# First FFN2 of a fused attention and SwiGLU kernel: one plain output tile instead of three, with the weight sums between the products of the first group

## The chip, the cores and the metric

The kernel runs on one core of one Trainium2 chip. The metric is the device time of one execution in microseconds; lower is better. Seven runs of the kernel before are given by their median, and one further execution was recorded by the hardware profiler.

## The reference, cut to what matters

```python
# q, k, v: (8 batches, 12 heads, 448 tokens, 64) in float32
scores = q @ k.T / sqrt(64) - log(448)
attn   = sigmoid(scores) @ v                      # per batch and head
x      = attn.transpose(0, 2, 1, 3).reshape(3584, 768)
g      = x @ w_gate                               # 768 x 1536
val    = x @ w_val
out    = (g * sigmoid(g) * val) @ w_out           # 1536 x 768, out is (3584, 768) float32
```

The last product, with `w_out`, is called FFN2 here. The two products before it, with the gate, are FFN1.

## The kernel before, in words

**Stages.** The eight batches are taken in four pairs `pb` = 0 to 3, each of 896 tokens. For each of the first three pairs TensorE runs 24 FFN1 units (`ffn1`, 12 blocks of 128 columns of d_ff for each of the two batches), and then FFN2 for the pair. The last pair has a different FFN1 (`ffn1_pair`), and then its FFN2. The attention of later batches is cut into steps (`attn_step`: three or four score chunks of one quad of heads, with `pv`, the product with v, of the quad before) and put between these units.

**FFN2.** A pair has 7 output tiles of 128 tokens by 768 columns. There are two ways to make them. `ffn2` makes one tile plainly: 12 blocks of d_ff by two halves of 384 columns, 24 matmuls. `ffn2_group` makes two tiles, g and g + 3, by a Strassen-like scheme with 7 products of 6 matmuls each, 42 matmuls for what would plainly be 48. The products are made in the order 1, 2, 6, 5, 7, 3, 4, in turn into the two banks of one PSUM tile, and after each VectorE moves the bank to an output buffer (`snap`, line 567) or adds it to what is there (`put`, line 573). The scheme needs sums of blocks of the hidden activations (`hS`, made on VectorE by `make_sums`, line 515) and sums of blocks of `w_out` (`wT`, made on VectorE by `w_sum(s, kind)`, line 484, s for one half of d_ff). Product 6 needs `wT` of kind 2, product 5 of kind 1, product 7 of kind 3 and product 4 of kind 4, each for s = 0 and, three matmuls later, for s = 1. Kind 2 is computed from kind 3, and kind 4 from kind 2. The weight sums are made once, in the FFN2 of pair 0, and used by all groups.

**The FFN2 of pair 0 before.** Its units are: `make_sums(99)` (all hidden sums still queued), `ffn2` of tile 6, four weight sums (s = 0), `ffn2` of tile 0, four weight sums (s = 1), `ffn2` of tile 3, and the groups g = 1 and g = 2. Pairs 1 to 3 have `ffn2` of tile 6 and three groups.

**Order of the work.** The whole order of instructions is fixed by the program: nothing is rescheduled. A list `units` holds the units with a planned duration each (`FU1`, `FU2`, `FU3`), and a running planned time `tcur` decides where each attention step is put: it goes ahead of the next unit once its due time `vtime` is reached. The due times are spread over the planned time up to `LAST`, the planned end of FFN1 of batch 5. Each `ffn1` of an odd batch makes some of the queued hidden sums on VectorE; how many (`budget`) depends on how soon an attention step follows.

**PSUM and buffers.** Eight banks form a ring of four tiles of two banks (`ring`). Each score chunk, each `pv`, each `ffn1`, each `ffn2` and each group takes the next tile of the ring (`Banked`). A matmul that starts a bank waits until the readers of that bank by its last user are done; the other bank does not matter. Output buffers `osb` come from a pool of four, and are stored by DMAs on SyncE's queue; the casts of q and k are on GpSimd.

## Time and profile before

| what | value |
| --- | --- |
| median of 7 runs | 410.87 us (409.89 to 413.54) |
| profiled execution, its own time | 409.85 us |
| its span from the first to the last instruction | 408.0 us |
| TensorE busy (share of the span) | 396.7 us (97%) |
| VectorE busy | 258.7 us (63%) |
| ScalarE busy | 231.7 us (57%) |
| GpSimd busy | 169.8 us (42%) |
| matmuls of plain FFN2 tiles, line 614 | 144 of 326 ns |
| matmuls of groups, line 556 | 462 of 326 ns |
| weight sums, line 484 | 8, seven of about 750 ns, one of 1485 ns |

The table counts 144 plain matmuls (six tiles of 24) and 462 in groups (eleven groups of 42). Matmuls overlap in TensorE's pipeline, so the mean of one is longer than the distance between two. The granted TensorE clock is 1.000 for the whole span.

### The profile page before, as it was taken

The page shows a single profiled execution, that of the slowest core. Times are in us where ns is not written, and L with a number is a line of the kernel's source. Part 1 is how long each engine was busy: PE and PEld are TensorE (multiplying, and loading weights), DVE is VectorE, ACT ScalarE, POOL GpSimd, SP SyncE. Part 2 cuts the span into 40 slices and gives each one's busy share as a digit, 9 for nine tenths or more (in the row PEclk, how much of TensorE's full clock was granted, in tenths as well). Part 3 has the DMA queues.
Part 4 walks back from the last instruction along what each step waited for, and adds up shares of the span by engine and source line. Part 5 has one row for each costly group of instructions (what it writes and reads, how often), then busy time and mean ns, then how long its engine had stood idle before and what let it go on. Part 6 is the DMA issues. An engine that isn't in the chain of part 4 may idle for free.

```text
span 408.0 us, 8021 instructions
## 1 busy us (share of the span) xinstructions
PE 396.7 (97%) x3158; PEld 206.2 (51%) x3158; DVE 258.7 (63%) x463; ACT 231.7 (57%) x333; POOL 169.8 (42%) x209
## 2 busy tenths in 40 slices
PE   7799999999999999999999999999999999999995
PEld 3444544545555444444555544445455555555563
DVE  2637647688955554767755555558786557777753
ACT  5966885744355667575444476685565435666000
POOL 3628042353433333331203043400039999999000
PEclk9999999999999999999999999999999999999999
DMA  8999956959899968872437897810002520000135
GB/s 260 251 249 251 236 95 119 199 119 211 213 207 269 218 158 154 170 141 100 112 80 169 232 174 164 181 34 15 1 2 53 141 80 0 2 1 0 40 83 148
DMA packets 59844, 54.38 MB, mean 133 GB/s; under 512 B 35744, under 2 KB 53280, under 8 KB 59808
## 3 DMA queue, kind: packets, MB, share of 16 engines
q0 software_dynamic: 18880, 30.94, 34.1%
q1 hardware_dynamic: 40496, 22.62, 24.8%
q8 instruction: 24, 0.39, 0.4%
q10 hardware_dynamic: 432, 0.33, 0.3%
q14 instruction: 12, 0.10, 0.1%
HBM read 47.19 MB, written 11.01 MB: 143 GB/s over the span
## 4 chain that ended last, share of the span: by engine, by line
PE 87%; DVE 5%; ACT 3%; DMA 3%; issue 1%; SPq 0%; POOL 0%; DVEq 0%; ACTq 0%
PE ps_D L296 39%; PE ps_D L556 19%; PE ps_D L403 11%; PE ps_D L230 8%; PE ps_D L262 6%; PE ps_D L614 4%; DMA v<-in_v_dram 2%; ACT pt L248 2%; DVE S L515 2%; DMA st<-in_q_dram 1%; PE ps_D L200 1%; DVE t L316 1%; DVE hT L320 1%; ACT pt L245 1%; DVE hT L428 0%
## 5 line engine op out<-in xcount | busy, mean ns | idle before, releaser
L248 ACT ACTIVATE pt<-ps_D,sb_t 128x896 f16<-128x896 f32 x148 | 140.1, 1017 | 74.6 <-PE ps_D L230 69.9
L296 PE MATMUL ps_D<-xT,wg 128*128 128x448 f16 x432 | 95.3, 353 | 0.1
L296 PE MATMUL ps_D<-xT,wv 128*128 128x448 f16 x432 | 94.8, 352 | 0.0
L181 POOL CAST c<-st 128x896 bf16<-128x896 f32 x41 | 38.3, 937 | 134.6 <-DMA st<-in_q_dram 84.7
L316 DVE TENSOR_TENSOR t<-ps_D,s 128x448 f16<-128x448 f32 x72 | 44.7, 622 | 58.6 <-ACT s L314 58.6
L296 PEld LDWEIGHTS <-wg 128*128 128x128 f16 x432 | 39.5, 98 | 44.9 <-issue 12.1
L296 PEld LDWEIGHTS <-wv 128*128 128x128 f16 x432 | 42.2, 98 | 39.5 <-issue 0.4
L314 ACT ACTIVATE s<-ps_D 128x448 f16<-128x448 f32 x72 | 39.5, 549 | 38.9 <-PE ps_D L296 28.3
L320 DVE SCALAR_TENSOR_TENSOR hT<-ps_D,t 128x448 f16<-128x448 f32 x72 | 45.0, 625 | 7.5
L230 PE MATMUL ps_D<-T,T 64*64 64x448 bf16 x644 | 44.4, 357 | 2.4 <-DVE T L206 1.2
L567 DVE TENSOR_SCALAR osb<-ps_D 128x384 f32<-128x384 f32 x43 | 24.0, 558 | 20.2 <-PE ps_D L556 19.0
L262 PE MATMUL ps_D<-pt,v 64*64 64x448 f16 x672 | 36.0, 350 | 0.4 <-DMA v<-in_v_dram 0.4
L556 PEld LDWEIGHTS <-S 128*128 128x128 f16 x264 | 25.8, 98 | 17.1
L556 PE MATMUL ps_D<-wT,S 128*128 128x384 f16 x198 | 34.0, 326 | 0.0
L230 PEld LDWEIGHTS <-T 64*64 64x64 bf16 x644 | 15.0, 105 | 25.1 <-issue 18.2
L271 DVE CAST xT<-ps_D 128x448 f16<-128x448 f32 x24 | 15.0, 625 | 19.8 <-PE ps_D L262 15.6
L573 DVE SCALAR_TENSOR_TENSOR osb<-ps_D,osb 128x384 f32<-128x384 f32 x33 | 18.4, 558 | 13.5 <-PE ps_D L556 13.5
L262 PEld LDWEIGHTS <-v 64*64 64x64 f16 x672 | 19.5, 107 | 13.2 <-issue 0.9
L556 PEld LDWEIGHTS <-hT 128*128 128x128 f16 x198 | 18.7, 98 | 14.6 <-issue 2.9
L276 DVE CAST xT<-ps_D 64x448 f16<-64x448 f32 x41 | 25.5, 621 | 0.7
L614 PE MATMUL ps_D<-wo,hT 128*128 128x384 f16 x144 | 24.4, 326 | 0.5 <-DVE hT L428 0.3
L556 PE MATMUL ps_D<-wo,hT 128*128 128x384 f16 x132 | 23.3, 326 | 0.0
(80 smaller groups left out, 427.5 us busy)
## 6 DMA issues: line engine op xcount, KB each, us to landing
out_dram<-osb SPq DMA_DIRECT2D x52, 192.0 KB, 2.9
st<-in_q_dram POOLq DMA_DIRECT2D x20, 448.0 KB, 6.0
st<-in_k_dram POOLq DMA_DIRECT2D x20, 448.0 KB, 7.3
v<-in_v_dram POOLq DMA_DIRECT2D x24, 224.0 KB, 5.2
wg<-in_moe_w_gate_dram POOLq DMA_DIRECT2D x4, 576.0 KB, 12.3
wv<-in_moe_w_val_dram POOLq DMA_DIRECT2D x4, 576.0 KB, 12.8
wo<-in_moe_w_out_dram POOLq DMA_DIRECT2D x4, 576.0 KB, 6.7
st<-in_q_dram SPq DMA_DIRECT2D x3, 448.0 KB, 7.6
```

The source lines that it names most:

```text
L181: eng.tensor_copy(out=t.rearrange("p c h d -> p h c d"), in_=st.rearrange("p h (c d) -> p h c d", c=C))
L230: nc.tensor.matmul(out=sc[w * 64:(w + 1) * 64, h2, :S], lhsT=kt[r, w * 64:(w + 1) * 64], rhs=qt[r, :, w * 64:(w + 1) * 64], start=True, st ...
L248: nc.scalar.activation(out=pt, in_=sc[:, :, :S], func=SIGM, bias=sb_t, scale=qkscale)
L262: nc.tensor.matmul(out=P[g:g + 64, h2, :S], lhsT=vt[r, h2, c * D:(c + 1) * D], rhs=pt[r, h2, :], start=(c == 0), stop=(c == C - 1),)
L276: done = [nc.vector.tensor_copy(out=o, in_=i) for o, i in halves[how:]]
L296: nc.tensor.matmul(out=D.t[:, i, :S], lhsT=(wg16, wv16)[i][f // FW][:, pr, cs], rhs=xT[(b, pr)], start=(pr == 0), stop=(pr == NP - 1),),
L314: D.read(nc.scalar.activation(out=s16, in_=D.t[:, 0, :S], func=SIGM), 0)
L316: D.read(nc.vector.tensor_tensor(out=t1, in0=D.t[:, 0, :S], in1=s16, op=MULT), 0)
L320: nc.vector.scalar_tensor_tensor(out=hT[(b // 2, f)][:, b % 2, :], in0=D.t[:, 1, :S], scalar=HSC, in1=t1, op0=MULT, op1=MULT),
L403: nc.tensor.matmul(out=D[kind].t[:, bank, :S], lhsT=l, rhs=r, start=(first and i == 0), stop=(i == NP // 2 - 1), skip_group_check=True,),
L556: nc.tensor.matmul(out=D.t[:, bank, :hw], lhsT=l, rhs=B_(i), start=(first and i == 0), stop=(i == HF - 1), skip_group_check=True,),
L614: nc.tensor.matmul(out=D.t[:, half, :hw], lhsT=h[:, m * 128:(m + 1) * 128], rhs=wo16[f // FW][:, f % FW, half * hw:(half + 1) * hw], start ...
```

## The change

In the FFN2 of pair 0, tiles 0 and 3 are no longer made plainly but by a group g = 0, as in the other pairs. The eight weight sums are spread differently: kinds 3 and 2 for both s go ahead of `ffn2` of tile 6, kind 1 for s = 0 goes behind it (and behind the attention step that follows it), and the other three go into the group g = 0, behind its products 2, 5 and 7. `ffn2_group` gets an argument for them. As the planned duration of the stage is different, the due times of the later attention steps are computed anew.

```diff
-    def ffn2_group(pb, g):
+    def ffn2_group(pb, g, between):
...
+        def extra(k):
+            if k in between:
+                w_sum(*between[k])
+
...
         mm(2, 1, True, True)
         put(1, o1, 0)
+        extra(2)
...
         mm(5, 1, True, False)
         o2 = osp.tile([128, DM], FP32, tag="osb", name="osb")
         snap(1, o2, 1)
+        extra(5)
         mm(7, 0, False, False)
         put(0, o2, 1)
+        extra(7)
...
         o_units = [(0.0, make_sums, (99,)), (FU2, ffn2, (pb, C - 1))]
+        between = {}
         if pb == 0:
 
-            ts = [(0.0, w_sum, (s, kind)) for s in range(2) for kind in (3, 2, 1, 4)]
-            o_units += ts[:4] + [(FU2, ffn2, (pb, 0))] + ts[4:] + [(FU2, ffn2, (pb, 3))]
-        for g in range(1 if pb == 0 else 0, 3):
-            o_units.append((FU3, ffn2_group, (pb, g)))
+            ts = [(0.0, w_sum, (s, kind)) for s in range(2) for kind in (3, 2)]
+            o_units = o_units[:1] + ts + o_units[1:] + [(0.0, w_sum, (0, 1))]
+            between = {2: (1, 1), 5: (0, 4), 7: (1, 4)}
+        for g in range(3):
+            o_units.append((FU3, ffn2_group, (pb, g, between if g == 0 else {})))
```

## The prediction

> **What bounds the kernel now.** I read the page first: TensorE (PE) is busy for 97% of the span, and the chain that ended last is PE for 87% of it. So PE time is end time, unless PE waits.

> ```profile
> span 408.0 us, 8021 instructions
> PE 396.7 (97%) x3158; PEld 206.2 (51%) x3158; DVE 258.7 (63%) x463; ACT 231.7 (57%) x333; POOL 169.8 (42%) x209
> PE 87%; DVE 5%; ACT 3%; DMA 3%; issue 1%; SPq 0%; POOL 0%; DVEq 0%; ACTq 0%
> ```

> An average hides stages, so next I read the chain of waits over the stage that is edited, FFN2 of pair 0, from 98 us (columns: start, length, what).

> ```profile
> 98.99 0.62 DVE hT L320
> 99.61 0.97 DVE S L515
> ...
> 102.05 0.08 DVE S L515
> 102.13 0.19 issue
> 102.33 0.56 DVE osb L627
> 102.89 0.04 issue
> 102.93 7.96 PE ps_D L614 x48
> 110.89 0.50 PE ps_D L230 x8
> ...
> 113.09 6.93 PE ps_D L556 x42
> ```

> At the entry of this stage the chain is on VectorE (DVE), not on PE. The last gate (L320) is followed by six hidden sums (L515), and only then by the move of tile 6 out of PSUM (L627); when that ends at 102.89, PE starts tile 0 at 102.93. From there to 298 us the chain is PE without a gap worth naming: what is lost here isn't made up later. The timeline of the same stage gives durations and what else DVE does:

> ```profile
> 102.33 1.01 DVE L627 TENSOR_SCALAR osb<-ps_D 128x384 f32<-128x384 f32 x2
> 102.93 7.96 PE L614 MATMUL ps_D<-wo,hT 128*128 128x384 f16 x48 [0.18 <-DVE osb L627]
> 103.26 0.75 DVE L484 TENSOR_TENSOR wT<-wo,wo 128x1152 f16<-128x1152 f16 x1
> 104.04 0.76 DVE L484 TENSOR_TENSOR wT<-wT,wo 128x1152 f16<-128x1152 f16 x1
> 104.72 0.75 DVE L484 TENSOR_TENSOR wT<-wo 128x1152 f16<-128x1152 f16 x1
> 109.02 1.12 POOL L181 CAST c<-st 128x896 bf16<-128x896 f32 x1 [1.18 <-DMA st<-in_k_dram]
> 109.26 1.49 DVE L484 TENSOR_TENSOR wT<-wo 128x1152 f16<-128x1152 f16 x1
> ```

> PE waited just 0.18 for L627. Why it waits at all: the ring has four PSUM tiles. Tile 6 takes one, the three score chunks of the attention step behind it the other three, and the next FFN2 unit takes tile 6's again. Weight sums (L484) start 0.68 after one another, 0.78 where one needs the one just before; the last row took 1.49 beside a GpSimd cast.

> [...] tile 6's matmuls end at 102.06, yet L627 comes at 102.33, right behind the sums. [...] 1.49 for a weight sum against 0.75, 1.04 for a hidden sum at 99.53 against 0.36, both beside a cast of 0.93 to 1.12; the 0.56 PSUM moves keep their length beside casts.

> **The change part by part.**
> 1. *Fewer matmuls.* Tiles 0 and 3 cost 48 plain matmuls, 7.96 in the chain; group 0 costs 42, 6.93 in the chain for group 1. On PE: **-1.03**.
> 2. *Four weight sums ahead of tile 6's move.* On DVE's queue they are now between the last hidden sum and the move; what is queued behind them is that move, and PE's group 0 waits for its first half, as it takes the same PSUM tile. They start at 102.33 (where L627 was) and go 0.78 + 0.68 + 0.78 + 0.68 = 2.92 until the move starts at 105.25 instead. No idle time of DVE can take them in: before 102.33 it is in the hidden sums without a gap. PE has the three score chunks to do until 102.75 and nothing more: group 0 starts at 105.25 + 0.56 + 0.04 = 105.85 instead of 102.93: **+2.92**.
> 3. *The other four sums, inside the group.* Products follow each other every 0.98; in group 1 the moves start 1.26, 2.16, 3.13, 4.1, 5.08, 6.05 and 7.03 after the first matmul. A move takes 0.56 and lets the next start after 0.47. With 105.85 as the start I lay the sums between: kind 1 (s=0) 106.19 to 106.94, ahead of a move due at 107.11; kind 1 (s=1) 108.47 to 109.22, needed by the second half of product 5 at 109.28; kind 4 (s=0) 110.42 to 111.17, needed at 111.71; kind 4 (s=1) 111.56 to 112.31, needed by the second half of product 4 at 112.20. Only the last is late: **+0.15**. The cover is thin: margins of 0.06 to 0.5.
> 4. *Locks with GpSimd.* Its casts started at 106.91 and 109.02, when their loads had landed. The first store of the stage (103.37) now leaves near 106.3[...]. The sum at 106.19 has 0.24 + 0.14 in hand, so it costs 0 to 0.55; the one at 108.47 has 0.06, so 0 to 0.87. Not shown by this trace; both ends kept, 0 to 1.4, and I take **+0.3**.
> 5. *Attention steps moved.* The planned stage is 25.36 before and 24.39 after, so due times shift by up to 0.97, and three steps (quad 13 both, quad 14 first) come one FFN1 unit later, in batch 3: two FFN1 units between steps all along instead of three and two. The same spacing in batch 2 (130 to 164 us) shows no PE gap. With 3 + 2 hidden sums in a stretch of two units and four chunks, DVE has 1.9 for x (0.62 + 1.26, L271 and L276), 2.7 for two gates (0.72 + 0.64 each), 1.9 for five sums of 0.38: 6.5, where PE takes 0.50 + 1.32 + 0.38 + 4.65 = 6.85 in the chain. Taken at 0, bounds -0.2 (nothing to gain: no gap there now) to +0.6. The casts, loads and transposes tied to these steps move with them; loads follow a whole quad ahead.
> 6. *SyncE's queue.* Step 10's transposes stay behind six stores; the last two now leave after group 0's last move, at about 113.7 instead of 112.35. They took 4.46 in issue and land within 6; their users start at 127.6: 0. Output buffers: four; group 1's second takes that of tile 6, whose store leaves near 106.3 and lands within 7.4 (the longest here), needed after 117: 0.

> Sum: -1.03 + 2.92 + 0.15 + 0.3 + 0 = **+2.3**. Against the profiled execution's own 409.85 (408.0 of span and 1.85 around it) that gives 412.2. The median shown, 410.87, is 1.02 above that execution, so for a median I forecast 410.87 + 2.3 = **413.2**. Half a percent, about what a measurement of this kernel can tell from no change, is 2.05: the forecast is just over it.

> **The rivals.**
> - *A, forecast: the move of tile 6 is late behind four sums.* +2.05 (no lock) to +3.0: 412.9 to 413.9. For it: the queue order and the 0.18 wait that is already there. Chance 0.57, 0.13 of it within half a percent.
> - *B, partly absorbed.* The sums go faster or later slack takes some: the entry to pair 2's FFN2 (298 to 307 us) is on DVE with hidden sums of 0.95 beside GpSimd, where phases can fall differently. +1 to +2: 411.9 to 412.9. Chance 0.15.
> - *C, not slower: the move isn't held up.* If PE doesn't need tile 6's bank when group 0 starts, only the saved matmuls remain, -1.03, and the 0.18 wait: 410.87 - 1.2 = 409.7. It decides if the move ends by 102.9, which needs another ring tile or the sums behind the move; the written order of both queues says neither. Here too belongs that the change doesn't act: the matmul count would have to stay. Chance 0.08.
> - *D, more than forecast.* Both locks (1.4 instead of 0.3) and stalls in batch 3 (0.6): +3.3 to +4.5, 414.2 to 415.4. Margins of 0.06 speak for it, the empty two-unit stretches of batch 2 against. Chance 0.20.

> **How the numbers follow.** Slower by over 0.5%: 0.44 of A, all of D and a little of B: 0.66. Within 0.5%: the rest of A, most of B, half of C: 0.30. Faster by over 0.5% (below 408.8) needs C with something more: 0.04. The range leaves out the far ends of C and D: 411.4 to 414.9.

> **What would show it.** In the profile after: 120 matmuls on the plain line and 504 in groups; a PE gap near 102.75 of about 3.1, released by DVE's move of tile 6; four weight sums in a row from 102.33; group 0 about 7.1 long, with a short wait ahead of its last three matmuls; from there PE without gaps, some 2.1 to 2.4 later than before. A gap under 1 near 102.75 proves step 2 wrong; a weight sum of 1.2 or more inside the group, or PE idle inside it of over 0.5, shows step 4; gaps between 164 and 204 us show step 5 wrong.

## The result, and the profile after

The changed kernel takes **418.96 us** (median of 12 runs, 414.69 to 421.99) where the kernel before takes 410.36 us (31 runs beside them, 409.57 to 418.58). The ratio is 1.0156, 95% interval 1.0116 to 1.0196: slower, as forecast, but by some 6 us more than the 413.2 of the prediction and outside its range of 411.4 to 414.9. The ratio leaves out the longest runs of both kernels, three of the 12 here, and is therefore smaller than that of the medians (1.021). The profiled execution took 418.31 us, with a span of 416.5 us; the changed kernel was recorded a second time later (416.25 us, span 414.5 us).

The page of the profile after, first execution: span, TensorE's share, granted clock in 40 slices of the span, and the chain that ended last.

```profile
span 416.5 us, 8013 instructions
PE 398.1 (96%) x3152; PEld 206.5 (50%) x3152; DVE 261.5 (63%) x466; ACT 231.8 (56%) x333; POOL 170.3 (41%) x209
PEclk9999999999899999999999999999999999999999
PE 80%; DMA 7%; DVE 5%; ACT 4%; issue 2%; POOL 0%; SPq 0%; DVEq 0%; ACTq 0%; POOLq 0%
```

The chain now has 7% of DMA where it had 3%, and one slice, at 104 to 115 us, has a lower clock (its digit is 8). The waits of TensorE between 100 and 210 us (engine and line, what was waited for: us in total, times, longest) give the rest:

```profile
PE ps_D L230 <- DMA T<-c: 5.0, 2, 3.3
PE ps_D L556 <- DVE osb L634: 2.4, 1, 2.4
```

Line 634 is the move of tile 6 (627 before), line 230 a score matmul of an attention step, T a transposed q or k of a quad of heads that a DMA on SyncE's queue makes from the cast c. The kernel before had 0.2 in this stretch, all of it for the move. The timeline of the edited stage:

```profile
101.89 0.75 DVE L484 TENSOR_TENSOR wT<-wo,wo 128x1152 f16<-128x1152 f16 x1
102.24 0.76 PE L230 MATMUL ps_D<-T,T 64*64 64x448 bf16 x12
...
104.14 0.76 DVE L484 TENSOR_TENSOR wT<-wT,wo 128x1152 f16<-128x1152 f16 x1
104.81 1.02 DVE L634 TENSOR_SCALAR osb<-ps_D 128x384 f32<-128x384 f32 x2
105.42 3.49 PE L556 MATMUL ps_D<-wo,hT 128*128 128x384 f16 x12 [2.42 <-DVE osb L634]
...
105.74 1.27 DVE L484 TENSOR_TENSOR wT<-wo 128x1152 f16<-128x1152 f16 x1
...
108.71 3.43 PE L556 MATMUL ps_D<-wT,S 128*128 128x384 f16 x18
...
114.18 0.57 PE L230 MATMUL ps_D<-T,T 64*64 64x448 bf16 x8
```

Four weight sums run from 101.89, then the move, then group 0 at 105.42: the forecast picture. But the first 12 matmuls of the group took 3.49, and the whole group 8.76 (105.42 to 114.18) instead of some 7.4. The view by stretches of 3 us says why. Its columns are stretch, length, busy us (and instructions) of PE, PEld, DVE, ACT and POOL, PEclk, DMA share and GB/s:

```profile
103.00:106.00 3.00, 0.58 (x4) 0.41 (x5) 2.96 (x6) 2.48 (x3) 0.53 (x1) 1.00 1.19 166
106.00:109.00 3.00, 3.00 (x11) 1.32 (x10) 1.62 (x3) 0.00 (x0) 1.91 (x3) 0.50 0.75 227
109.00:112.00 3.00, 3.00 (x19) 1.76 (x18) 2.53 (x5) 0.00 (x0) 1.54 (x3) 0.94 0.79 141
```

TensorE was granted half its clock just behind the gap (0.50): in this record from 105.97 to 109.39 us, so for 3.41 us. The stage ends 114.18 - 110.89 = 3.29 later than before. Of the span's 8.5, 5.0 are still open, and they are the waits for T. The chain of waits from there:

```profile
116.49 0.03 SPq L188
116.51 0.03 issue
116.54 15.58 DMA T<-c
...
132.26 0.47 POOL c L181
...
134.85 13.36 DMA T<-c
148.21 0.04 issue
148.25 0.57 PE ps_D L230 x8
```

Quad 10's transposes (line 188) leave SyncE at 116.54 and need 15.58 to land; in the kernel before they left at 113.59 and landed within 6.5. TensorE stands for 1.71 for them at 131 to 132.7. The next cast on GpSimd, quad 12's, reuses a buffer that these transposes read, so it comes at 132.26 instead of 126.98, and quad 13's loads come behind it. Quad 11's transposes stand behind the stores of the last group and leave at 133.40 and 134.85, again beside loads; the second takes 13.36, and TensorE stands once more, 3.26. There was no slack for it: in the kernel before, quad 11's second transpose landed at 139.44, and the scores that read it started at 139.78. What is different in the DMAs between 112 and 136 us shows in the list of issues (KB each, median us to landing). After:

```profile
st<-in_q_dram POOLq DMA_DIRECT2D x2, 448.0 KB, 10.2
st<-in_k_dram POOLq DMA_DIRECT2D x2, 448.0 KB, 13.7
T<-c SPq DMA_TRANSPOSE x4, 14.0
```

Before, the same window:

```profile
st<-in_k_dram POOLq DMA_DIRECT2D x3, 448.0 KB, 7.1
st<-in_q_dram POOLq DMA_DIRECT2D x2, 448.0 KB, 6.7
T<-c SPq DMA_TRANSPOSE x6, 6.8
```

Loads and transposes are both 1.5 to 2 times as slow, though the windows don't hold quite the same ones. From 120 to 130 us all DMAs of the core together moved 120 GB/s, in the kernel before 241. In the kernel after, GpSimd issues quad 12's loads at 115.58 to 117.02 and SyncE the transposes at 116.54: they run beside each other. In the kernel before the transposes left at 113.59, 5.8 ahead of the loads at 119.37.

### The profile page after: what moved, and what is told of

It is laid out like the page before. It is cut to its first block, busy times and chain, and to the rows that moved or that the text cites. A ratio compares the mean times of both kernels' runs of the same rounds, so it can differ in the third digit from the quotient of the medians.

```text
span 416.5 us, 8013 instructions
## 1 busy us (share of the span) xinstructions
PE 398.1 (96%) x3152; PEld 206.5 (50%) x3152; DVE 261.5 (63%) x466; ACT 231.8 (56%) x333; POOL 170.3 (41%) x209
## 4 chain that ended last, share of the span: by engine, by line
PE 80%; DMA 7%; DVE 5%; ACT 4%; issue 2%; POOL 0%; SPq 0%; DVEq 0%; ACTq 0%; POOLq 0%
PE ps_D L296 36%; PE ps_D L556 17%; PE ps_D L403 11%; PE ps_D L230 7%; DMA T<-c 7%; PE ps_D L262 6%; ACT pt L248 3%; PE ps_D L621 2%; DVE S L515 1%; PE ps_D L718 1%; DVE t L316 1%; PE ps_D L200 1%; DVE hT L320 1%; DVE wT L484 1%; ACT pt L245 1%
## 5 line engine op out<-in xcount | busy, mean ns | idle before, releaser
L181 POOL CAST c<-st 128x896 bf16<-128x896 f32 x41 | 38.3, 940 | 143.8 <-DMA st<-in_q_dram 81.2
L230 PE MATMUL ps_D<-T,T 64*64 64x448 bf16 x644 | 44.4, 357 | 7.4 <-DMA T<-c 5.0
L320 DVE SCALAR_TENSOR_TENSOR hT<-ps_D,t 128x448 f16<-128x448 f32 x72 | 45.0, 625 | 7.9 <-PE ps_D L230 0.5
L567 DVE TENSOR_SCALAR osb<-ps_D 128x384 f32<-128x384 f32 x47 | 26.2, 558 | 20.8 <-PE ps_D L556 19.4
L556 PEld LDWEIGHTS <-S 128*128 128x128 f16 x288 | 28.4, 98 | 19.1 <-issue 0.7
L556 PE MATMUL ps_D<-wT,S 128*128 128x384 f16 x216 | 37.4, 328 | 0.0
L271 DVE CAST xT<-ps_D 128x448 f16<-128x448 f32 x24 | 15.0, 624 | 25.4 <-PE ps_D L262 18.0
L556 PEld LDWEIGHTS <-hT 128*128 128x128 f16 x216 | 20.8, 99 | 19.3 <-issue 6.9
L230 PEld LDWEIGHTS <-T 64*64 64x64 bf16 x644 | 14.9, 105 | 30.3 <-issue 18.0
L573 DVE SCALAR_TENSOR_TENSOR osb<-ps_D,osb 128x384 f32<-128x384 f32 x36 | 20.1, 557 | 14.9 <-PE ps_D L556 14.9
L556 PE MATMUL ps_D<-wo,hT 128*128 128x384 f16 x144 | 26.8, 338 | 2.4 <-DVE osb L634 2.4
L276 DVE CAST xT<-ps_D 64x448 f16<-64x448 f32 x41 | 25.5, 622 | 0.7
L174 POOL DMA_DIRECT2D v<-in_v_dram x24 | 18.0, 750 | 13.9 <-PE ps_D L230 12.7
```

The source lines that it names most:

```text
L181: eng.tensor_copy(out=t.rearrange("p c h d -> p h c d"), in_=st.rearrange("p h (c d) -> p h c d", c=C))
L230: nc.tensor.matmul(out=sc[w * 64:(w + 1) * 64, h2, :S], lhsT=kt[r, w * 64:(w + 1) * 64], rhs=qt[r, :, w * 64:(w + 1) * 64], start=True, st ...
L276: done = [nc.vector.tensor_copy(out=o, in_=i) for o, i in halves[how:]]
L320: nc.vector.scalar_tensor_tensor(out=hT[(b // 2, f)][:, b % 2, :], in0=D.t[:, 1, :S], scalar=HSC, in1=t1, op0=MULT, op1=MULT),
L556: nc.tensor.matmul(out=D.t[:, bank, :hw], lhsT=l, rhs=B_(i), start=(first and i == 0), stop=(i == HF - 1), skip_group_check=True,),
L567: nc.vector.tensor_scalar(out=o, in0=D.t[:, bank, :hw], scalar1=HREC, scalar2=None, op0=MULT), bank
```

## The experiments

**Theories.** Three things were held to make up the +8.5: the gap of steps 1 to 3 of the prediction (some +2); half clock behind that gap (1.3 to 1.7); and transposes beside loads (5.0). Rivals: that the moved attention steps, weight sums slowed beside GpSimd's casts (step 4's locks; in the kernel before one took 1.49 instead of 0.75), or the group's late stores by themselves do it. The expectations number the theories in the order in which they came up. In the edits below, `plan` is the kernel's table of what goes with each attention step (n, part): `casts`, `trans` (transposes) and `fetch` (loads) of a quad.

### The sums ahead of the move, without the group

e4: the kernel before, three plain tiles, but with the changed kernel's four sums ahead of tile 6.

```diff
-ts = [... for s in range(2) for kind in (3, 2, 1, 4)]
-o_units += ts[:4] + [(FU2, ffn2, (pb, 0))] + ts[4:] + [(FU2, ffn2, (pb, 3))]
+ts = [... for kinds in ((3, 2), (1, 4)) for s in range(2) for kind in kinds]
+o_units = o_units[:1] + ts[:4] + o_units[1:]
+o_units += ts[4:6] + [(FU2, ffn2, (pb, 0))] + ts[6:] + [(FU2, ffn2, (pb, 3))]
```

> The kernel before, with its three plain tiles, but with the weight sums of kinds 3 and 2 for both halves put ahead of tile 6's move, as in the change (the other four go behind the moves of tiles 6 and 0). Theory: TensorE waits 2.4 to 2.9 us ahead of tile 0, and the clock drops for 3.4 us: +2.7 for the wait and +1.7 for the clock against the kernel before, 414 to 415; with only two stores instead of four just ahead of quad 10's transposes these may still meet the loads of quad 12, which adds up to 5. Rival 2b (the group with its four stores is what hurts): no more than +1, 411.

Measured: 415.65 us (412.80 to 424.35), ratio 1.0084 [1.0052, 1.0115]. TensorE's waits, and two stretches of the view by stretches, of the profiled execution (span 414.3):

```profile
PE ps_D L614 <- DVE osb L627: 3.1, 1, 3.1
```

```profile
106.00:109.00 3.00, 2.74 (x9) 1.28 (x9) 2.01 (x4) 0.00 (x0) 1.26 (x2) 0.50 1.01 354
109.00:112.00 3.00, 3.00 (x11) 1.35 (x10) 0.00 (x0) 0.00 (x0) 2.80 (x4) 0.50 0.43 76
```

The wait grew by 2.9, as step 2 said. Half clock held for 6.83 us, from 105.42; TensorE starts again at 106.26, and its 48 matmuls then take 10.89 instead of 7.96, so 2.9 is lost to the clock. With 0.4 that this execution had lost before (tile 6 starts at 98.39 instead of 98.00) that is 408.0 + 0.4 + 2.9 + 2.9 = 414.2 of the span's 414.3. The sums ahead of the move alone make the gap, and the clock behind it cost as much here as the gap grew, 2.9 each. There were no waits for T here.

### The gap and the transposes taken away, one at a time and together

e1: the changed kernel with quad 10's transposes put one step earlier, ahead of group 0's stores in SyncE's queue.

```diff
-(8, 4): ((casts, 10),),
-(9, 0): ((trans, 10), (fetch, 11)),
+(8, 4): ((casts, 10), (trans, 10)),
+(9, 0): ((fetch, 11),),
```

> The changed kernel, with the two DMA transposes of quad 10 queued on SyncE right behind tile 6's two stores, ahead of the four stores of group 0. Theory 1 (in the changed kernel these transposes, issued at 116.5 us, run beside the loads of quad 12, and both slow down; TensorE then waits 1.7 and 3.3 us for transposes): the transposes go out near 107 to 109 us, land well ahead of need, the waits for quad 10's and 11's transposes fall from 5.0 to under 1 us, and the time is 4 to 5 us below the changed kernel, 413 to 415. Rival 2 (what is lost is lost at the entry to the stage, in the wait for VectorE and the slow clock behind it): no change from the changed kernel, about 418.

Measured: 413.67 us (411.83 to 414.15), ratio 1.0067 [1.0045, 1.0089]; profiled span 410.0. TensorE's waits between 100 and 210 us:

```profile
PE ps_D L556 <- DVE osb L634: 2.9, 1, 2.9
PE ps_D L556 <- DVE wT L484: 0.2, 1, 0.2
```

There is no wait for T. The gap was there (2.9), but this execution kept the full clock, and its group took 7.45 (105.38 to 112.83): 1.3 less than the changed kernel's, which is the price of half clock there. The median lies 1.8 above this execution (410.0 and 1.85 around it); the mean clock of the other runs was 0.990 to 0.996, so they probably had it: as an estimate from the 3.41 us in the changed kernel, one such stretch takes 3.41 / 2 / 410 = 0.004 off the mean.

e3: the changed kernel with 40 repeats of the third chunk's score matmuls, which write the same values again, ahead of group 0, so that TensorE isn't idle while VectorE makes the sums. e8: e3 and e1 together.

```diff
+if part and part[-1] == (8, C - 1):
+    for _ in range(10):
+        for w in range(2):
+            for h2 in range(2):
+                nc.tensor.matmul(out=scs[-1][2].t[...], lhsT=kt[...], rhs=qt[...], start=True, stop=True)
```

> The changed kernel, with 40 matmuls added that repeat the scores of the third chunk of the attention step ahead of group 0 (the same result is written again), so that TensorE is busy while VectorE makes the four weight sums. Theory 4 (the half clock from 105.4 to 108.8 us comes from TensorE's idle 2.4 us, and costs 3.41 / 2 = 1.7): the clock stays at 1.000 in this stretch, group 0 takes 7.0 to 7.5 us instead of 8.8, and the time is some 1.7 below the changed kernel if the later transposes are unchanged, more if the earlier end of group 0 also lets them out of the loads' way. Rival 5 (the half clock is a matter of chance in an execution): it is seen here too, and nothing is gained.

> The changed kernel with both remedies, quad 10's transposes first and TensorE filled with 40 repeated matmuls while it would wait. Theory (wait, half clock and transposes are all there is): only the later start of group 0, some 2.9 us, less the six matmuls, is left: +2.0 against the kernel before, 412 to 412.7, with little spread, and no time at half clock near 105 us. Rival: more than 413.5, so that something else is left.

Measured: e3 412.54 us (411.57 to 413.31), ratio 1.0048 [1.0030, 1.0065]; e8 412.37 us (411.71 to 413.45), 1.0052 [1.0036, 1.0068]. TensorE's waits of e8 between 100 and 210 us are one line:

```profile
PE ps_D L556 <- DVE osb L634: 0.8, 1, 0.8
```

Without the slow clock (the mean of this execution is 1.000) and without the transposes' wait, e8 is 412.37 - 410.43 = 1.94 above the kernel before that ran beside it. Steps 1 to 4 had forecast 2.34. What e3 did not explain is why filling the gap also took away the waits for T: its transposes left SyncE at 117.43, later than in the changed kernel. The last group of experiments is about that.

e6: e1 with the attention steps in the order of the kernel before (the planned length of the stage kept as it was).

```diff
-o_units.append((FU3, ffn2_group, ...))
+o_units.append((FU3 + (3 * FU2 - FU2 - FU3 if between and g == 0 else 0.0), ffn2_group, ...))
```

> The changed kernel with quad 10's transposes ahead of group 0's stores (as in the run above that did this alone), and with the planned duration of group 0 set so that the later attention steps have the order of the kernel before. Theory (the moved attention steps cost nothing): as the run with the transposes first alone, 413 to 414, within 0.3%. Rival 6 (the closer steps in batch 3 cost something): 1 us or more below it.

Measured: 413.25 us, ratio 1.0072 [1.0053, 1.0092] against e1's 1.0067: the moved steps cost nothing that can be told.

e2: the changed kernel, with GpSimd waiting until quad 10's transposes have landed before it issues quad 12's loads.

```diff
+    for n in (8,):
+        plan[(n + 1, 4)] = plan[(n + 1, 4)][:1] + ((landed, n + 2),) + plan[(n + 1, 4)][1:]
```

> The changed kernel, with the loads of quad 12 on GpSimd held until the transposes of quad 10 have landed (one small copy on GpSimd that reads the transposed tile); the transposes stay where they are on SyncE, behind group 0's four stores. Theory 1 (it is the company of the loads that makes the transposes slow): each transpose lands within 6 us instead of 15.6 and 13, and the waits for them fall from 5.0 to under 1 us: 413 to 415. Rival 3 (it is the late place on SyncE's queue alone, behind four stores in a row): the transposes are issued as late as in the changed kernel and TensorE waits as long, 418, or longer, as the loads are late too.

Measured: 417.25 us (413.13 to 423.60), ratio 1.0118 [1.0075, 1.0161]. The profiled execution (span 411.3) has half clock for 3.41 us and no wait for T, with the transposes landed within 5.6. But the loads left only at 123.1, and the six runs spread by over 10 us: two of them lie in the forecast 413 to 415, the others above it. Those were not recorded, so what they waited for is open, and this run alone doesn't show what the meeting costs.

### The transposes alone, in the kernel before

e5: the kernel before, with quad 10's transposes put behind group 1's stores. e12: the kernel before, with the edit of e1.

```diff
 # e5
-(9, 0): ((trans, 10), (fetch, 11)),
+(9, 0): ((fetch, 11),),
+plan[(9, 4)] = ((casts, 11), (trans, 10), (fetch, 12))
```

> The kernel before, unchanged but for the place of quad 10's two transposes: they go behind group 1's four stores on SyncE's queue, so they are issued near 122 us instead of 113.6 and run beside the loads of quad 12 (issued from 119.4). Theory 1 (transposes that run beside loads are slow, and TensorE waits for them): they take 8 to 16 us instead of about 5, the scores that need them at 127.6 wait for 3 to 10 us, and the time is 3 us or more above the kernel before, 413.5 to 420, with no wait for VectorE's move and no half clock ahead of it. Rival 3 (a late place alone): they land within 6 us, near 128, and the wait is under 1: 411.

> The kernel before with nothing changed but quad 10's transposes, which go right behind tile 6's stores, near 107 to 109 us instead of 113.6. Theory 9 (this early place shifts the later loads and transposes against each other): waits for quad 12's transposes appear, 412 to 416. Rival 10 (the early place is harmless, and what went wrong with the sums spread came from TensorE's coming earlier): as the kernel before, 410.4.

Measured: e5 415.12 us (414.08 to 423.18), ratio 1.0117 [1.0092, 1.0142]; e12 411.13 us, 1.0015 [0.9998, 1.0033]. In e5 (span 415.0) a late transpose is enough, without group 0 and without the gap:

```profile
PE ps_D L230 <- DMA T<-c: 4.3, 1, 4.3
```

Half clock for 6.83 us sets in during that wait, at 130.20, and TensorE works from 132.37, so the 4.65 us of it in which it works cost some 2.3, an estimate (half of 4.65); 4.3 + 2.3 = 6.6 of the 7.0 by which the span grew. e12 says that the early place itself is worth nothing in a kernel that has no wait for T.

### The sums elsewhere

e11: no sum ahead of the move; those for s = 0 in FFN1 of batch 1, where VectorE has time (from 62 to 98 us it is busy for 26.3 of 36 us in the kernel before), those for s = 1 behind the move and inside the group. e7: the same with the transposes early as in e1.

```diff
 snap(0, o1, 0)
+extra(1)
...
+EARLY = {4: ((0, 1),), 7: ((0, 3), (0, 2)), 10: ((0, 4),)}
...
+if b == 1 and f in EARLY:
+    units += [(0.0, w_sum, a) for a in EARLY[f]]
...
-o_units = o_units[:1] + ts + o_units[1:] + [(0.0, w_sum, (0, 1))]
-between = {2: (1, 1), 5: (0, 4), 7: (1, 4)}
+o_units += [(0.0, w_sum, (1, 3))]
+between = {1: (1, 2), 2: (1, 1), 5: (1, 4)}
...
```

> A version meant to be better: group 0 as in the change and quad 10's transposes first, but no weight sum ahead of tile 6's move. The four sums of the first half of d_ff go into idle time of VectorE during FFN1 of batch 1; those of the second half go behind tile 6's move and into group 0, behind products 1, 2 and 5. Theory: the wait for the move is back to 0.2 or 0.3, the clock stays, no transposes are waited for, and what is left is the six matmuls less (-1.0) and waits of 0.3 to 0.5 inside the group for sums: 0.5 below the kernel before, 409.5 to 410.5. Rival 7 (the group itself costs something that the plain tiles do not): 411.5 or more.

> The version with the weight sums spread, with quad 10's transposes behind group 0's stores as in the change. There TensorE was 0.7 us ahead of the kernel before at the end of group 0, and then waited 3.8 us for quad 12's transposes, which ran beside quad 13's loads and took 12. Theory 9 (the earlier place of quad 10's transposes has shifted the later loads and transposes against each other): here the wait is gone, 409.5 to 410.5. Rival 10 (the loads and transposes have no slack for a TensorE that comes earlier, wherever quad 10's go): 414 to 417 again.

Measured: e7 416.35 us, ratio 1.0145 [1.0124, 1.0167]; e11 410.40 us (14 runs, 409.45 to 416.61), 1.0009 [0.9983, 1.0035]. TensorE's waits of e7 (span 414.0), 100 to 210 us:

```profile
PE ps_D L230 <- DMA T<-c: 3.8, 1, 3.8
PE ps_D L556 <- DVE osb L635: 0.2, 1, 0.2
```

The forecast of 409.5 to 410.5 was missed. In e7 the gap is gone, and the group ends 0.7 ahead of the kernel before. But the second of quad 11's transposes (the expectation of e11 calls them quad 12's) left at 131.0 beside quad 13's loads at 130.35 and took 12.0, and half clock for 6.83 us set in during the wait for it. e11, which differs from e7 only in the place of quad 10's transposes, is without waits for T in its profile and as fast as the kernel before. So even without the gap the 1.03 of step 1 did not show in the time: 410.40 against 410.41 of the kernel before that ran beside it, though the interval leaves room for a gain of up to 0.7. The record shows where a part of it went: inside the group TensorE waits 0.5 for a move that stands behind a weight sum of 1.40 instead of 0.75. No version beat the kernel before.

### Why the filled kernels don't wait for the transposes

e9: e3 with 80 repeats instead of 40, so that the group, its stores and the transposes are as late as in the changed kernel. e10: e9 with early transposes.

```diff
 # e9 (e13: 30); e10 has the early transposes of e1 besides
-    for _ in range(10):
+    for _ in range(20):
```

> The changed kernel with 80 repeated matmuls ahead of group 0 instead of 40, so that TensorE is busy past the point at which VectorE is ready: group 0 starts some 1.5 us later than it must, at full clock, and ends about when it ends in the changed kernel or later; quad 10's transposes stay behind its stores. Theory 1b (what decides is how late group 0's stores let the transposes out, not the clock or an idle TensorE as such): the waits for transposes are back in most runs, 416 to 420. Rival 8 (it is the idle or slow TensorE that goes with the waits for transposes, in some way that the trace does not show): no waits, 414.

> The same 80 repeated matmuls, with quad 10's transposes ahead of group 0's stores: the control of the run above. Theory 1b: only the 1.5 us more of filling against 40 matmuls and the transposes first (412.4) are seen: 413.5 to 414.2, with little spread. Under rival 8 the same.

Measured: e9 412.91 us (14 runs, 13 of them at or under 414.1), ratio 1.0056 [1.0029, 1.0082]; e10 413.15 us, 1.0069 [1.0046, 1.0092]. The chain of e9:

```profile
103.01 3.78 PE ps_D L705 x80
106.79 6.56 PE ps_D L556 x39
```

e9's group ended at 114.00, its transposes left at 116.30, as late as in the changed kernel, and TensorE did not wait for them. That the lateness of the stores alone does it was thereby refuted. What differed was GpSimd: in e9 it issued quad 12's loads at 117.85, behind the transposes, in the changed kernel at 115.58, ahead of them. The loads follow casts that follow earlier loads, and the phase of that chain differs by 1 to 3 us from one execution to the next, ahead of the edited stage already: in the two records of the changed kernel quad 9's loads leave at 87.17 and at 89.91. So the theory became: what decides is whether the transposes meet the loads. Three last runs put it to the test: e13 (e3 with 120 repeats) makes the transposes later without a gap; e14 makes the loads later and leaves the gap; e15 is the changed kernel recorded again.

```diff
 # e14
+space = one.tile([128, 512], BF16, tag="space", name="space")
+def spaced(k):
+    for _ in range(k):
+        nc.gpsimd.tensor_copy(out=space, in_=warm)
+plan[(9, 4)] = ((casts, 11), (spaced, 5), (fetch, 12))
```

> The changed kernel with 120 repeats of the third chunk's score matmuls ahead of the first group: TensorE is not idle there, but the group starts some 1.9 us later than with 80 repeats (108.7 instead of 106.8), and so quad 10's transposes leave SyncE near 118.2. Theory 11 (what decides is whether those transposes are issued before or after quad 12's loads, whose time varies by 1 to 3 us between executions): with the loads at 115.6 to 117.9 the transposes are behind them in most executions, the waits for transposes come back, 416 to 420 us. Rival 8 (the waits come with an idle TensorE and its slower clock, however late the transposes are): no waits, 412.9 + 1.9 = 414.8 us.

> The changed kernel with five small copies on GpSimd between quad 11's casts and quad 12's loads, so that these loads are issued about 2 to 2.5 us later (near 118 instead of 115.6), behind quad 10's transposes at 116.5. The gap of 2.4 us ahead of the first group and the slow clock behind it stay. Theory 11: the transposes run alone, no waits for them at 127 to 150 us, 413 to 415 us, unless the later loads hold up quad 12's own casts and transposes. Rival 8: waits for transposes as in the changed kernel, 417 to 420 us.

> The changed kernel as it is, profiled once more, for a second reading of the same race. Theory 11: if quad 10's transposes are issued after quad 12's loads, waits for transposes of 3 us or more and a span of 414 us or more; if before them by more than 1 us, none, and a span near 411.5 to 412.5 us. Rival 8: the waits are there in both orders, as long as the gap ahead of the first group is followed by the slow clock.

Measured: e13 418.12 us (415.07 to 422.55), ratio 1.0163 [1.0109, 1.0217]; **e14 413.59 us** (412.56 to 416.01), ratio 1.0078 [1.0049, 1.0106]; e15 415.88 us (415.22 to 419.74), 1.0148 [1.0104, 1.0191]. GpSimd's timeline of e14:

```profile
117.72 3.33 POOL L859 COPY space<-warm 128x512 bf16<-128x512 bf16 x5
120.99 0.72 POOL L174 DMA_DIRECT2D v<-in_v_dram  x1
```

The waits of e14 between 100 and 210 us, and what the profile says of quad 10's transposes:

```profile
PE ps_D L556 <- DVE osb L634: 3.0, 1, 3.0
```

```profile
L188 SPq DMA_TRANSPOSE T<-c x2: 1243/1272/1302, 116.9 to 118.3; - x2
DMA to landing us min/median/max: 3.6/4.1/4.5
```

The gap (3.0) and half clock behind it (0.63 at 106 to 109, 0.80 at 109 to 112) are there, the transposes leave at 116.89, later than in the changed kernel's first record, and land in 4.5 because the loads come only at 120.99. No wait for T is left. e15 shows the other side, waits first:

```profile
PE ps_D L556 <- DVE osb L634: 3.0, 1, 3.0
PE ps_D L230 <- DMA T<-c: 2.6, 2, 2.0
PE ps_D L556 <- DVE wT L484: 0.6, 1, 0.6
```

```profile
106.00:109.00 3.00, 2.30 (x15) 1.39 (x15) 2.49 (x6) 0.15 (x1) 0.80 (x1) 1.00 1.06 374
```

In e15 the clock stayed full (1.00) behind a gap of 3.0, and the waits for T (2.6) came all the same, so they don't need the slow clock. Over all recorded kernels in which quad 10's transposes can meet these loads:

| kernel | transposes leave | loads of quad 12 leave | difference | transposes land within | TensorE's waits for T |
| --- | --- | --- | --- | --- | --- |
| before | 113.59 | 119.37 | -5.8 | 6.5 | 0 |
| e2 | 116.49 | 123.10 | -6.6 | 5.6 | 0 |
| e11 | 113.92 | 118.16 | -4.2 | 7.0 | 0 |
| e14 | 116.89 | 120.99 | -4.1 | 4.5 | 0 |
| e9 | 116.30 | 117.85 | -1.6 | 6.7 | 0 |
| e15 | 116.85 | 117.23 | -0.4 | 15.1 | 2.6 |
| e3 | 117.43 | 116.53 | +0.9 | 10.3 | 0 |
| after | 116.54 | 115.58 | +1.0 | 15.6 | 5.0 |
| e13 | 118.41 | 117.16 | +1.3 | 12.6 | 0 |
| e4 | 119.34 | 117.10 | +2.2 | 7.8 | 0 |
| e5 | 122.57 | 120.08 | +2.5 | 8.1 | 4.3 |

In this table transposes that leave over 1.5 ahead of the loads land within 7. Within 1.3 of the loads they took 10.3 to 15.6; further behind, about 8. Later in the same records the border is softer: in the kernel before, transposes that left from 129.80 beside loads at 129.97 took at most 8.2, in e7 those at 129.20 and 131.00 beside loads at 130.35 took 5.8 and 12.0. So in these records transposes that met loads could land late (up to 15.6), but didn't always (from 5.8 on). Whether TensorE then waits depends on when it asks: in e3 at 130.54 and in e13 at 132.83, 1 to 3 us after theirs had landed; in e5 they had only left at 122.57. That e13's other runs lie at 415.6 to 422.6 fits waits that come and go, but none of them was recorded. The clock can't be all of it: the two longest, 421.95 and 422.55, had a mean clock of 0.996 and 0.995, which is at most some 2 us of the 7 above the recorded run. e15's expectation had waits of 3 or none; at a difference of -0.4 it had 2.6, so the border isn't as sharp as the theory put it.

It is not the transposes alone that moved. The last cast ahead of quad 12's loads waits for the last load of quad 11. GpSimd's timeline, before and in e15:

```profile
118.49 0.93 POOL L181 CAST c<-st 128x896 bf16<-128x896 f32 x1 [2.42 <-DMA st<-in_k_dram]
```

```profile
116.35 0.94 POOL L181 CAST c<-st 128x896 bf16<-128x896 f32 x1 [0.28 <-DMA st<-in_k_dram]
```

That load left at 111.52 before and at 111.54 in e15, but took 6.9 before and 4.8 in e15. Before, two stores (from 112.38) and quad 10's transposes (from 113.59) left beside it; in e15 the next store left at 114.36. So quad 12's loads came 2.1 us sooner in e15 (3.8 in the first record, where quad 11's loads had left 1.7 sooner as well), while the transposes came 3 us later. That the missing stores and transposes are what made the load faster is my guess from these times; it was not tested by itself.

**What goes with half clock.** The records also tell when a gap was followed by half clock. In the first record of the changed kernel the times at which the granted clock changes lie 29, 1 and 90 times 3.413 us apart, in the kernel before 118 times, and the half clocks of the experiments between 100 and 210 us lasted 3.41 or 6.83. So each record is read here as a fixed row of stretches of 3.413 us, laid from its own changes of the clock, and the place of a gap in it can be read off. The table has, for each gap of over 2.4 us between 100 and 210 us, the stretch in which TensorE was least busy:

| record | gap | stretch | TensorE busy in it | clock in the next stretch |
| --- | --- | --- | --- | --- |
| e7 | 139.25 to 143.07 | 138.46 to 141.87 | 0.79 | half |
| e2 | 102.91 to 105.36 | 102.23 to 105.64 | 0.95 | half |
| after | 103.00 to 105.42 | 102.56 to 105.97 | 0.99 | half |
| e14 | 102.74 to 105.76 | 103.35 to 106.76 | 1.00 | half |
| e4 | 103.15 to 106.26 | 102.01 to 105.42 | 1.14 | half |
| e5 | 128.04 to 132.37 | 126.78 to 130.19 | 1.26 | half |
| after | 144.99 to 148.25 | 143.52 to 146.93 | 1.47 | full |
| e1 | 102.49 to 105.38 | 103.53 to 106.94 | 1.56 | full |
| e15 | 103.67 to 106.70 | 102.08 to 105.49 | 1.59 | full |
| e6 | 103.05 to 106.13 | 101.24 to 104.65 | 1.81 | full |

Where the gap lay for the most part in one stretch, with 1.26 us of work or less in it, the next one ran at half clock; where a gap as long was split more evenly between two, with 1.47 or more in each, the clock stayed. Half clock lasted a second stretch where TensorE was busy for 1.24 to 2.57 us of the first (e5, e7, e4), and ended where it was busy for all of it (after, e2, e14). So the length of the gap alone didn't decide (2.42 was followed by half clock, 3.26 was not), and where it falls in the row differs between executions. The border between 1.26 and 1.47 was seen in these ten gaps only: in the first 10 us, with other work, e11 and e12 (mean clock 0.990 and 0.994) went to half clock behind stretches with 1.63 and 1.76.

## Why the prediction was wrong

The direction was right, and so was the mechanism of steps 1 to 5. The sum lacked two terms: transposes that meet loads, which step 6 put at 0, and the half clock behind the gap, which step 2 left out.

- **Steps 1 to 3** held in kind. The move came behind four sums in a row and TensorE waited 2.42 (3.0 in the second record) for it, where 3.1 was forecast: the move started at 104.81, right behind the sums, though tile 6's matmuls had ended at 102.30. The 2.34 of steps 1 to 4 stands against 1.94 in e8, where the repeated matmuls keep the clock up and the transposes leave early. Step 2 was the one too dear: from the start of tile 6 to that of group 0 it is 7.46 in e8 and 4.93 before, 2.5 more and not 2.92. In the first record none of the six hidden sums met a cast (about 0.36 each; before, one took 1.04), so the weight sums started at 101.89 instead of 102.33. Group 0 at full clock took 7.40 in e8 (105.68 to 113.08), against 7.08 forecast by step 3 and 7.38 with step 4.
- **Step 2 lacked a term.** It priced the gap at its own length. Of the seven records with a gap of 2.4 to 3.1 us ahead of the stage, four had half clock behind it: for 3.41 us, which cost 1.3 in the first record, or for 6.83 (e4: 2.9). A gap of 2.42 was followed by half clock, while 3.0 in e15 and 2.9 in e1 were not; what tells them apart is how much work they leave in one stretch of the row above, 0.99 us against 1.59 and 1.56. The trace of the kernel before, with a clock of 1.000 for the whole span, shows nothing of this, and I gave the forecast gap of 3.1 no term for it.
- **Step 4.** Its 0 to 1.4 was my estimate, from casts of 0.93 and margins of 0.38 and 0.06. One of the two sums named did meet a cast, in the first record the one at 105.74 (1.27 instead of 0.75, beside a cast from 105.47), in e15 the one at 109.32 (1.45). In the first record it hid behind the slow clock; in e15, e3 and e6 TensorE waited 0.6 for a sum, in e1 0.2. The 0.3 taken lies between these.
- **Step 5** at 0 is confirmed by e6 (1.0072 against 1.0067).
- **Step 6 is the step that failed.** "They took 4.46 in issue and land within 6; their users start at 127.6: 0" took the landing time from a trace in which the next loads come 5.8 later (and read it short: the first of the two took 6.5). The change moved them 3 us towards the loads of GpSimd's queue and brought these loads 2 us and more towards them, and I didn't ask what runs beside them there. They landed in 15.6 and 15.1, and TensorE waited 5.0 and 2.6. Nor did I look at the margin of the next quad, which was 0.34 in the kernel before. I had put "loads follow a whole quad ahead" in step 5 and left it at that; the loads' chain itself shifts by up to 3 us between executions, so this margin had to be taken as a chance, not as a time.
- **The rivals.** D was nearest in time and wrong in its cause: neither two sums of group 0 held by casts nor stalls in batch 3 (and its terms sum to 4.0 at most, not to 4.5). No case had transposes and loads that take longer beside each other.

The pieces add up for both records of the changed kernel. First: 3.29 at the stage's end and 5.0 of waits make 8.3 of the span's 8.5. Second: the stage ends at 114.49, 3.6 later (0.9 of it lost ahead of the stage, as tile 6 starts at 98.92 instead of 98.00), and the waits are 2.6: 6.2 of 6.5.

What isn't settled: why transposes issued within 1.3 us of the loads took up to 15.6 us, and the loads in the same window 10.2 and 13.7, and why not in other places (8.2 at most in the kernel before, from 129.80); and what the longest runs of the changed kernel (421 to 422 us) hold beyond the two records. Their mean granted clock is among the lowest of the twelve (0.984 to 0.988 against 0.996 in the first record). As an estimate from these figures and the 3.41 us, that is three to four stretches at half clock where the first record has one; none of these runs was recorded.

## What to carry to other kernels

When a step on a DMA queue moves by even 3 us, look at what the other queues issue at its new place: the same transposes landed within 6.5 us in the kernel before and within 15.6 beside loads, so a landing time was good only beside the traffic it was read beside. When traffic moves away from a transfer, look at what follows that transfer too: here a load with fewer stores and transposes beside it landed in 4.8 instead of 6.9, and the next loads left 2.1 sooner. Price a gap on TensorE with the possible half clock behind it (0, 1.3 or 2.9 us here), not with its length alone. A saving of 1 us on a full engine is lost at once if the work that makes it possible is put in front of something this engine waits for: 1.03 saved stood here against waits of 2.4 to 3.1.
